# One exponential a tile in a decode kernel's attention, its weights spread to eight masked heads by a VectorE product

## The chip, the cores and the metric

The kernel runs on one core of a Trainium2 chip. The metric is the device time of one execution in microseconds. Engines are named as in the profile: PE is TensorE, DVE is VectorE, ACT is ScalarE, POOL is GpSimd, SP is SyncE, which here issues nearly all DMA transfers.

## What is computed

The kernel is one decode step for four sequences: a layernorm of x (4 x 640), attention over a cache, a small gated MLP beside it, and the sum of the three. All inputs and the output are bf16.

```python
xn = _layernorm(x)                                # x: 4 x 1 x 640
q = (xn @ wq).reshape(4, 1, 32, 128).transpose(0, 2, 1, 3)
scores = jnp.einsum('bhqd,bhkd->bhqk', q, k_cache) * 128 ** -0.5
p = softmax(scores)                               # over 4096 keys
o = jnp.einsum('bhqk,bhkd->bhqd', p, v_cache)     # caches: 4 x 32 x 4096 x 128
attn = o.transpose(0, 2, 1, 3).reshape(4, 1, 4096) @ wo
z = gelu(xn @ w_in); z1, z2 = z[..., :864], _layernorm(z[..., 864:])
mlp = (z1 * (w_sp * z2 + b_sp)) @ w_out
out = x + attn + mlp
```

Each of the 128 pairs of sequence and head has its own query, keys and values. The two caches are 134 MB each and are read once, so nearly all bytes (282 MB) are cache.

## The kernel before, in words

**Tiles.** A tile is eight heads of one sequence: 16 tiles (`NT`), in four head groups (`HG`) of four sequences (`Bsz`). A tile's K is 8 x 4096 rows of 128 numbers, laid out as 128 partitions ("lanes") with 256 rows each (`NC`), 8.39 MB; V is the same. A lane's 256 rows all belong to one head: 16 lanes (`LN`) for each of the eight heads (`HT`).

**Scores.** In tile i, K is worked on in four quarters (`NU`), each in four steps. `product(i, u)` (L402) multiplies a quarter in place on DVE by the lane's query, `fold(i, u)` (L411) adds its upper half of 64 columns to the lower, `sums(i, u)` (L420) adds the 64 columns up to 8 on PE by eight matmuls with an identity, and `row_sums(i, u)` (L431) adds the last 8 on DVE and writes 64 scores a lane into `s_sb`, a tile with **one** buffer. The query of the next tile is spread over the lanes by `stage_q` (L383, L388, L396).

**Softmax.** For tile i-1, during tile i: `lane_max` (L440) on DVE, `turn_max` (L445) on PE, `head_max` (L450) on DVE, `spread_max` (L461) on PE, and `bias` (L468) on DVE, which makes `nb`: for each lane eight numbers, the negative scaled maximum of head h, and -1e30 more (`off`) where the lane isn't of head h. `exps` (L480) then runs eight activations on ACT, one for each head, over all lanes: head h's weights are the exponentials on its own 16 lanes and zero on the other 112. They go to `pm[:, :, h]`, 128 lanes x 256 rows x 8 heads in bf16, so that one activation's outputs lie eight elements apart. Each also gives the row sum of its head (`accum_out`, into `acc`).

**Weighted values.** `weighted(i-1)` (L495) is 64 matmuls on PE: four rows by eight heads of `pm` are the weights, and four rows of V are the moving data; PE holds four groups of 32 columns. `take` (L505) copies the result on ACT, and `diag` (L515) picks with `pick` the pieces that belong together (a row's own position c among four and a head h: row c * 8 + h of the 32). `pm` has two buffers (pool `pmp`).

**After each group of four tiles.** `group_den` (L525, L529) adds the row sums over the lanes, `group_rows` (L533, L537) divides and spreads the rows over heads (`wide`), `group_turn` (L551, L559) transposes on PE. At the very end `group_proj` (L564) multiplies by `wo`, which was loaded last.

**What sets the order.** The order on PE, DVE, ACT and SP is the order of the calls in the loop (`manual_schedule`). K has two buffers, V one. In pass i of the loop SP issues V(i) (`load_v`, L128), which must wait until `weighted(i-1)` has read V(i-1), and after it K(i+2) (`load_k`, L122), which must wait until `sums(i, 3)` has read K(i). SP issues in order, and the transfers of its queue run in order. V of the last tile (`v_last`) goes into K's pool, and `wo` (L143) into V's.

Of the kernel before, what the change touches and what calls it, by code (L numbers as in the profile page):

```python
# [9 lines left out]
FP32 = mybir.dt.float32  # L10
BF16 = mybir.dt.bfloat16
ACT = mybir.ActivationFunctionType
ALU = mybir.AluOpType
AX = mybir.AxisListType

OFF = -1.0e30


@with_exitstack
def kernel(  # L20
# [14 lines left out]
    nc = tc.nc  # L35
    P = nc.NUM_PARTITIONS
    Bsz, Sq, D = A_x.shape
    _, H, S, Dh = A_k_cache.shape
# [4 lines left out]
    scale_qk = float(Dh) ** -0.5  # L43
# [3 lines left out]
    HT = 8  # L47
    HG = H // HT
    NT = HG * Bsz
    LN = P // HT  # L50
    NC = HT * S // P
# [17 lines left out]
    const = ctx.enter_context(tc.tile_pool(name="const", bufs=1))  # L69
    kp = ctx.enter_context(tc.tile_pool(name="kp", bufs=2))  # L70
    vp = ctx.enter_context(tc.tile_pool(name="vp", bufs=1))
    work = ctx.enter_context(tc.tile_pool(name="work", bufs=1))
    small = ctx.enter_context(tc.tile_pool(name="small", bufs=2))
    pmp = ctx.enter_context(tc.tile_pool(name="pmp", bufs=2))
    PSUM = bass.MemoryType.PSUM
    ps_s = ctx.enter_context(tc.tile_pool(name="ps_s", bufs=2, space=PSUM))
    ps_pv = ctx.enter_context(tc.tile_pool(name="ps_pv", bufs=2, space=PSUM))
# [7 lines left out]
    def v_slot(name):  # L85
# [21 lines left out]
        out=w_out_sb[:, 0:NFF, :], in_=B_w_out[0 : NFF * P].rearrange("(p k) n -> p k n", k=NFF)  # L107
# [42 lines left out]
    ident_f = const.tile([P, P], FP32)  # L150
# [5 lines left out]
    ones_col = const.tile([P, 1], FP32)  # L156
# [9 lines left out]
    for i in range(NSTAT):  # L166
# [9 lines left out]
        out=xn_bf,  # L176
        in0=x_bf,
        scalar1=mv[:, 0:1],
# [20 lines left out]
    for half in range(2):  # L199
# [6 lines left out]
        )  # L206


    off = const.tile([P, HT], FP32)
    nc.vector.tensor_reduce(  # L210
        out=off[:], in_=ident_f[:].rearrange("p (h l) -> p h l", h=HT), axis=AX.X, op=ALU.add
    )
    nc.vector.tensor_scalar(
        out=off[:], in0=off[:], scalar1=1.0, scalar2=-OFF, op0=ALU.subtract, op1=ALU.mult
    )
    nc.vector.tensor_reduce(
        out=pick[:, :, GW - HT : GW],
        in_=ident_f[:].rearrange("p (j c h) -> p c h j", c=CB, h=HT),
        axis=AX.X,
        op=ALU.add,  # L220
    )
    row_head = const.tile([ROWS, HT], FP32)
    nc.vector.tensor_reduce(
        out=row_head[:],
        in_=ident_f[:ROWS, :ROWS].rearrange("p (b h) -> p h b", h=HT),
        axis=AX.X,
        op=ALU.add,
    )
    row_batch_f = work.tile([ROWS, Bsz], FP32)
    nc.vector.tensor_reduce(  # L230
# [24 lines left out]

    GM = 2 * NFC * Bsz
    gm = {}
    gm_t = small.tile([P, 4 * GM + NFC * Bsz], FP32, tag="two_k", name="gm_t", bufs=1)
    for n, name in enumerate(("zz", "gw", "gt", "gz")):
        gm[name] = gm_t[:, n * GM : (n + 1) * GM].rearrange(  # L260
            "p (t k b) -> p t k b", t=2, b=Bsz
# [139 lines left out]
    def product(i, u):  # L401
        nc.vector.tensor_tensor(  # L402
            out=part(i, u),
            in0=part(i, u),
            in1=qbcs[i][:, None, :].to_broadcast([P, UC, Dh]),
            op=ALU.mult,
        )

    def fold(i, u):
        t = part(i, u)  # L410
        nc.vector.tensor_tensor(  # L411
            out=t[:, :, 0:HD2], in0=t[:, :, 0:HD2], in1=t[:, :, HD2:Dh], op=ALU.add
        )
# [50 lines left out]
        maxes[i] = nb_ps  # L464

    def bias(i):
        nb = small.tile([P, HT], FP32, name="nb")
        nc.vector.scalar_tensor_tensor(  # L468
            out=nb[:], in0=maxes[i][:], scalar=scale_qk, in1=off[:], op0=ALU.mult, op1=ALU.add
        )  # L470
        maxes[i] = nb

    def exps(i):
        hg, b = divmod(i, Bsz)
        if b == 0:
            accs[hg] = small.tile([P, Bsz, HT], FP32, name="acc")
        nb, s_sb, a = maxes.pop(i), scores.pop(i), accs[hg]
        pm = pms[i] = pmp.tile([P, NC, HT], BF16, tag="pm", name="pm")
        for h in range(HT):
            nc.scalar.activation(  # L480
                out=pm[:, :, h],
                in_=s_sb[:],
                func=ACT.Exp,
                bias=nb[:, h : h + 1],
                scale=scale_qk,
                accum_out=a[:, b, h : h + 1],
            )

    def weighted(i, c0=0, c1=NC):
        if c0 == 0:  # L490
            pvs[i] = ps_pv.tile([P, CB * Dh], FP32, tag="pv", name="pv")
        v_nat, pm = v_tiles[i], pms[i]
        for n in range(c0 // CB, c1 // CB):
            j = n % CG
            nc.tensor.matmul(  # L495
                out=pvs[i][j * GW : (j + 1) * GW, :],
                lhsT=pm[:, n * CB : (n + 1) * CB, :],
                rhs=v_nat[:, n * CB : (n + 1) * CB, :],
                start=(n < CG),
                stop=(n >= NB - CG),  # L500
            )

    def take(i):
        es[i] = small.tile([P, CB, Dh], FP32, tag="two_k", name="e", bufs=1)
        nc.scalar.copy(  # L505
            out=es[i][:], in_=pvs.pop(i)[:].rearrange("p (c d) -> p c d", d=Dh)
        )
# [13 lines left out]
            )  # L521

    def group_den(hg):
        den = ps_m.tile([ROWS, 1], FP32, tag="m", name="den")
        nc.tensor.matmul(  # L525
            out=den[:], lhsT=accs.pop(hg)[:], rhs=ones_col[:], start=True, stop=True
        )
        rdens[hg] = small.tile([ROWS, 1], FP32, name="rden")
        nc.vector.reciprocal(out=rdens[hg][:], in_=den[:])  # L529

    def group_rows(hg):
        o_n = small.tile([ROWS, Dh], BF16, name="o_n", bufs=1)
        nc.vector.tensor_scalar(  # L533
            out=o_n[:], in0=o_ps.pop(hg)[:], scalar1=rdens.pop(hg)[:], scalar2=None, op0=ALU.mult
        )
        wide = small.tile([ROWS, WJ, HT, LN], BF16, tag="two_k", name="wide", bufs=1)
        nc.vector.tensor_tensor(  # L537
            out=wide[:],
            in0=o_n[:].rearrange("r (m j) -> r j m", j=WJ)[:, :, None, :].to_broadcast(
                [ROWS, WJ, HT, LN]  # L540
            ),
            in1=row_head[:, None, :, None].to_broadcast([ROWS, WJ, HT, LN]),
            op=ALU.mult,
        )
        oTs[hg] = wide
# [26 lines left out]
    def at(i, fn, *args):  # L572
        if 0 <= i < NT:
            fn(i, *args)
# [6 lines left out]
    with tc.manual_schedule(engines={E.PE, E.DVE, E.Activation, E.SP}):  # L581
        stage_q(0)
        gmlp()
        load_v(0, v_slot("v_nat"))
        for i in range(NT):
            product(i, 0)
            fold(i, 0)
            at(i - 1, row_sums, NU - 1)
            at(i - 1, lane_max)
            group(i - 2, group_rows)  # L590
            sums(i, 0)
            at(i - 1, turn_max)
            group(i - 2, group_turn)
            product(i, 1)
            at(i - 1, head_max)
            at(i - 1, spread_max)
            fold(i, 1)
            at(i - 1, bias)
            at(i - 1, exps)
            at(i + 1, stage_q)  # L600
            sums(i, 1)
            row_sums(i, 0)
            product(i, 2)
            fold(i, 2)
            sums(i, 2)
            row_sums(i, 1)
            at(i - 1, weighted)
            if i == 0:
                pass
            elif i < NT - 1:  # L610
                load_v(i, v_slot("v_nat"))
            else:
                load_wo()
            at(i - 1, take)
            product(i, 3)
            fold(i, 3)
            sums(i, 3)
            row_sums(i, 2)
            if i + 2 < NT:
                load_k(i + 2)  # L620
            elif i + 2 == NT:
                load_v(NT - 1, k_slot("v_last"))
            at(i - 1, diag)
            group(i - 1, group_den)
        L = NT - 1
        row_sums(L, NU - 1)
        lane_max(L)
        group(L - 1, group_rows)
        turn_max(L)
        head_max(L)  # L630
        spread_max(L)
        bias(L)
        exps(L)
        for c0, c1 in zip(V_CUTS, V_CUTS[1:]):
            weighted(L, c0, c1)
        take(L)
        group_den(HG - 1)
        group_proj(0)
        diag(L)
        group_rows(HG - 1)  # L640
        group_proj(1)
        group_turn(HG - 1)
        group_proj(2)
        for j0, j1 in zip(WO_CUTS, WO_CUTS[1:]):
            group_proj(HG - 1, j0, j1)

        res = small.tile([P, NOH], BF16, tag="two_k", name="res", bufs=1)
        out_v = out.flatten_outer_dims()
        r0, r1 = slice(0, Bsz), slice(OG, OG + Bsz)
        nc.scalar.copy(out=res[r0], in_=out_ps[r0])  # L650
        nc.vector.tensor_copy(out=res[r1], in_=out_ps[r1])
        nc.scalar.dma_start(out=out_v[:, 0:NOH], in_=res[r0])
        nc.sync.dma_start(out=out_v[:, NOH:D], in_=res[r1])
# [30 lines left out]
```

## Time and profile before

| | us |
|---|---|
| three timed runs | 721.27, 718.67, 721.26; median 721.26 |
| the profiled execution, its own time | 722.45 |
| its span in the profile | 720.5 |
| busy: PE / PE weight loads / DVE / ACT / POOL | 310.7 / 129.2 / 491.3 / 172.7 / 1.0 |
| read from memory | 282.24 MB, 392 GB/s over the span |
| share of DMA queue 1 (that of SP) | 91.9% of 16 engines' span |

The span runs from the first to the last instruction of the program on the core; the execution's own time has some 2 us around it. Busy time counts an engine's instructions alone. A line of the groups reads: source line, engine, operation, output <- inputs with their shapes (partitions x elements) and how many; then busy us in all and mean ns of one; then the idle time ahead of them and what ended it. A line of the waits reads: who waited <- for whom: us in all, times, longest. A line of a time line reads: start us, us, engine, line, operation; in brackets the idle time ahead of it and what ended that. A line of windows has the stretch, its length, the busy time of each engine with its number of instructions, the granted PE clock, the DMA share and GB/s.

### The profile page before, as it was taken

What the parts mean: (1) busy time and instruction counts of PE and PEld (TensorE: products, weight loads), DVE (VectorE), ACT (ScalarE), POOL (GpSimd) and SP (SyncE); (2) the same over time, 40 slices, a digit from 0 to 9 for tenths busy, and PEclk for the clock granted to TensorE, in tenths of its full rate; (3) what the DMA queues carried; (4) which work ended last, traced back from release to release, by engine and by line L of the source; (5) the groups of instructions that cost most, each with busy time, mean ns of one, the idle gap of its engine ahead of it and who ended that gap; (6) DMA issues with size and microseconds to landing.
All of it is one profiled execution on the core that took longest, in us unless ns stands there. A gap on an engine that the chain in (4) does not pass through costs nothing.

```text
span 720.5 us, 4972 instructions
## 1 busy us (share of the span) xinstructions
PE 310.7 (43%) x2089; PEld 129.2 (18%) x2089; DVE 491.3 (68%) x291; ACT 172.7 (24%) x317; POOL 1.0 (0%) x8
## 2 busy tenths in 40 slices
PE   1513445252626327252634525272542617254256
PEld 1401112021202102020211202030120202022023
DVE  1259869474958849486876849497784849678441
ACT  0200130505041050503123050502205050320542
POOL 0000000000000000000000000000000000000000
PEclk9996558575866657585576758566575756767578
DMA  9999958999899997999899997999999897999981
GB/s 379 444 426 440 419 233 350 407 456 415 354 407 407 416 455 295 407 463 411 350 407 466 409 451 303 411 408 437 433 387 429 353 463 295 407 463 407 395 361 66
DMA packets 6498, 282.56 MB, mean 392 GB/s; under 512 B 736, under 2 KB 1100, under 8 KB 1484
## 3 DMA queue, kind: packets, MB, share of 16 engines
q1 hardware_dynamic: 6456, 282.24, 91.9%
q8 instruction: 16, 0.26, 0.1%
q14 instruction: 6, 0.05, 0.0%
q10 hardware_dynamic: 20, 0.01, 0.0%
HBM read 282.24 MB, written 0.01 MB: 392 GB/s over the span
## 4 chain that ended last, share of the span: by engine, by line
DVE 37%; DMA 34%; ACT 14%; PE 12%; issue 1%; SPq 0%; DVEq 0%
DMA k_nat<-in_A_k_cache_dram 34%; DVE k_nat L402 22%; ACT pm L480 14%; DVE k_nat L411 11%; PE s_ps L420 6%; PE pv L495 5%; DVE s_sb L431 3%; DVE wide L537 1%; DVE m L440 1%; PE out_ps L564 0%; PE o_ps L515 0%; DVE nm L450 0%; DVE o_n L533 0%; DVE nb L468 0%; SPq L109 0%
## 5 line engine op out<-in xcount | busy, mean ns | idle before, releaser
L402 DVE TENSOR_TENSOR k_nat<-k_nat,qbc 128x8192 bf16<-128x8192 bf16 x64 | 282.6, 4416 | 28.1 <-DMA k_nat<-in_A_k_cache_dram 28.1
L420 PE MATMUL s_ps<-k_nat,ident 128*128 128x512 bf16 x512 | 198.9, 559 | 181.3 <-DVE k_nat L411 181.3
L480 ACT ACTIVATE pm<-s_sb,nb 128x256 bf16<-128x256 f32 x128 | 149.8, 1582 | 223.3 <-DVE nb L468 223.3
L411 DVE TENSOR_TENSOR k_nat<-k_nat 128x4096 bf16<-128x4096 bf16 x64 | 146.4, 2287 | 1.7
L431 DVE TENSOR_REDUCE s_sb<-s_ps 128x64 f32<-128x512 f32 x64 | 43.9, 686 | 143.5 <-ACT pm L480 141.5
L420 PEld LDWEIGHTS <-ident 128*128 128x128 bf16 x512 | 65.2, 130 | 292.9 <-issue 264.0
L388 PE MATMUL qbc_ps<-ident,q_l 128*128 128x128 bf16 x16 | 4.5, 284 | 157.7 <-ACT q_l L383 157.7
L480 ACT ACTIVATION_READ_ACCUMULATOR pm<-s_sb,nb 128x1 f32 x128 | 63.0, 493 | 0.0
L505 ACT COPY e<-pv 128x512 f32<-128x512 f32 x16 | 9.4, 586 | 220.9 <-PE pv L495 215.3
L495 PE MATMUL pv<-v_nat,pm 128*32 128x512 bf16 x960 | 61.6, 414 | 0.0
L495 PEld LDWEIGHTS <-pm 128*32 128x32 bf16 x1024 | 27.2, 105 | 53.6 <-issue 23.9
L388 PEld LDWEIGHTS <-q_l 128*128 128x128 bf16 x16 | 1.7, 104 | 159.3 <-ACT q_l L383 159.1
L461 PE MATMUL nb_ps<-nm,ones_row 1*128 1x8 f32 x32 | 8.5, 336 | 35.9 <-DVE nm L450 35.9
L515 PE MATMUL o_ps<-e,pick 128*32 128x128 f32 x128 | 16.9, 275 | 0.0
L529 DVE RECIPROCAL rden<-den 32x1 f32<-32x1 f32 x4 | 0.6, 156 | 23.1 <-PE den L525 23.1
L461 PEld LDWEIGHTS nb_ps<-nm,ones_row 1*128 1x128 f32 x32 | 7.1, 275 | 44.2 <-DVE nm L450 29.8
L515 PEld LDWEIGHTS o_ps<-e,pick 128*32 128x32 f32 x128 | 12.8, 109 | 6.4 <-issue 6.4
L383 ACT COPY q_l<-qT 128x128 bf16<-128x128 bf16 x16 | 8.7, 543 | 17.4 <-DVE qT L251 17.4
L559 ACT CAST oT<-t_ps 128x32 bf16<-128x32 f32 x4 | 0.7, 186 | 45.2 <-PE t_ps L551 45.2
L396 ACT CAST qbc<-qbc_ps 128x128 bf16<-128x128 f32 x16 | 4.3, 266 | 29.1 <-PE qbc_ps L388 29.1
L251 DVE CAST qT<-q_ps 128x128 bf16<-128x128 f32 x1 | 0.3, 292 | 14.9 <-PE q_ps L243 14.9
L495 PE MATMUL pv<-v_last,pm 128*32 128x512 bf16 x64 | 5.5, 519 | 9.7 <-ACT pm L480 9.7
(81 smaller groups left out, 80.8 us busy)
## 6 DMA issues: line engine op xcount, KB each, us to landing
wq<-in_A_wq_dram SPq DMA_DIRECT2D x1, 5120.0 KB
v_last<-in_A_v_cache_dram SPq DMA_DIRECT2D x1, 4096.0 KB, 29.9
v_last<-in_A_v_cache_dram SPq DMA_DIRECT2D x2, 2048.0 KB, 34.5
wo<-in_A_wo_dram SPq DMA_DIRECT2D x3, 1280.0 KB
w_sb<-in_B_w_in_dram SPq DMA_DIRECT2D x1, 2160.0 KB, 20.1
w_sb<-in_B_w_out_dram SPq DMA_DIRECT2D x1, 960.0 KB, 22.6
wo<-in_A_wo_dram SPq DMA_DIRECT2D x1, 640.0 KB, 13.1
wo<-in_A_wo_dram SPq DMA_DIRECT2D x1, 320.0 KB, 11.9
```

The costliest lines, as they stand in the source:

```text
L383: nc.scalar.copy(out=q_l[:], in_=qT[:, HT * hg : HT * (hg + 1), b : b + 1].to_broadcast([P, HT, LN]),)
L402: nc.vector.tensor_tensor(out=part(i, u), in0=part(i, u), in1=qbcs[i][:, None, :].to_broadcast([P, UC, Dh]), op=ALU.mult,)
L411: nc.vector.tensor_tensor(out=t[:, :, 0:HD2], in0=t[:, :, 0:HD2], in1=t[:, :, HD2:Dh], op=ALU.add)
L420: nc.tensor.matmul(out=s[:], lhsT=ident[:], rhs=t[:, :, g * RW : (g + 1) * RW], start=(g == 0), stop=(g == n - 1),)
L431: nc.vector.tensor_reduce(out=scores[i][:, u * UC : (u + 1) * UC], in_=sums_ps.pop((i, u))[:], axis=AX.X, op=ALU.add,)
L440: nc.vector.tensor_reduce(out=m1[:], in_=scores[i][:], axis=AX.X, op=ALU.max)
L461: nc.tensor.matmul(out=nb_ps[:], lhsT=ones_row[:], rhs=maxes[i][:], start=True, stop=True)
L480: nc.scalar.activation(out=pm[:, :, h], in_=s_sb[:], func=ACT.Exp, bias=nb[:, h : h + 1], scale=scale_qk, accum_out=a[:, b, h : h + 1],)
L495: nc.tensor.matmul(out=pvs[i][j * GW : (j + 1) * GW, :], lhsT=pm[:, n * CB : (n + 1) * CB, :], rhs=v_nat[:, n * CB : (n + 1) * CB, :], sta ...
L505: nc.scalar.copy(out=es[i][:], in_=pvs.pop(i)[:].rearrange("p (c d) -> p c d", d=Dh))
L515: nc.tensor.matmul(out=o_ps[hg][:], lhsT=pick[:, c, GW - HT - HT * b : 2 * GW - HT - HT * b], rhs=e[:, c, :], start=(b == 0 and c == 0), s ...
L537: nc.vector.tensor_tensor(out=wide[:], in0=o_n[:].rearrange("r (m j) -> r j m", j=WJ)[:, :, None, :].to_broadcast([ROWS, WJ, HT, LN]), in1 ...
```

## The change

The lane-by-head mask moves from the exponential's bias to a product on DVE.

- The mask `own` (1 where the lane is of head h, else 0) takes the place of `off`. `own_c` is the same in bf16, each value four times.
- `bias` multiplies the eight maxima by `own` and adds them up (`accum_out`), which gives one number a lane: the maximum of its own head.
- `exps` is one activation over all lanes, into `p` (128 x 256 bf16, outputs in neighbouring elements), with one row sum a lane.
- `own_heads` is new: a DVE product of `p`, repeated for eight heads, and `own_c`, repeated for 64 blocks of four rows, into `pm`, now laid out as blocks x heads x four rows. In pass i it stands between `product(i, 2)` and `fold(i, 2)`, on DVE; at the end it follows the last exponential.
- `weighted` reads the four rows by eight heads of a block from neighbouring elements; `pick` follows the new order (row h * 4 + c of the 32).
- `group_den` spreads the lane's row sum over the heads with `own` before its matmul.
- `group_rows` writes `o_n` in the order in which `wide` reads it, and `row_head` is bf16 and spread over the 16 lanes once, at the start, so that `wide`'s product has bf16 operands in steps of one.
- The pool of `pm` goes from two buffers to one; the tiles of the tag `two_k` (`gm_t`, `e`, `wide`, `res`) go from one buffer to two.

The order of all other calls is as it was. On ACT 112 of 128 exponentials are gone; DVE has 21 instructions more; PE and SP have as many as before, in the same order.

```diff
-    pmp = ctx.enter_context(tc.tile_pool(name="pmp", bufs=2))
+    pmp = ctx.enter_context(tc.tile_pool(name="pmp", bufs=1))
...
-    nc.vector.tensor_scalar(
-        out=off[:], in0=off[:], scalar1=1.0, scalar2=-OFF, op0=ALU.subtract, op1=ALU.mult
-    )
+    own_c = const.tile([P, HT, CB], BF16)
+    nc.vector.tensor_copy(out=own_c[:], in_=own[:, :, None].to_broadcast([P, HT, CB]))
...
+    row_head = const.tile([ROWS, HT, LN], BF16)
+    nc.vector.tensor_copy(
+        out=row_head[:], in_=row_head_f[:, :, None].to_broadcast([ROWS, HT, LN])
     )
...
     def bias(i):
-        nb = small.tile([P, HT], FP32, name="nb")
+        nb = small.tile([P, 1], FP32, name="nb")
+        nb_h = small.tile([P, HT], FP32, name="nb_h")
         nc.vector.scalar_tensor_tensor(
-            out=nb[:], in0=maxes[i][:], scalar=scale_qk, in1=off[:], op0=ALU.mult, op1=ALU.add
+            out=nb_h[:],
+            in0=maxes[i][:],
+            scalar=scale_qk,
+            in1=own[:],
+            op0=ALU.mult,
+            op1=ALU.mult,
+            accum_out=nb[:],
         )
...
-        for h in range(HT):
-            nc.scalar.activation(
-                out=pm[:, :, h],
...
+        probs[i] = small.tile([P, NC], BF16, name="p")
+        nc.scalar.activation(
+            out=probs[i][:],
+            in_=scores.pop(i)[:],
+            func=ACT.Exp,
+            bias=maxes.pop(i)[:],
+            scale=scale_qk,
+            accum_out=accs[hg][:, b : b + 1],
+        )
+
+    def own_heads(i):
+        pm = pms[i] = pmp.tile([P, NB, HT, CB], BF16, tag="pm", name="pm")
+        nc.vector.tensor_tensor(
+            out=pm[:],
+            in0=probs.pop(i)[:]
+            .rearrange("p (n c) -> p n c", c=CB)[:, :, None, :]
+            .to_broadcast([P, NB, HT, CB]),
+            in1=own_c[:, None, :, :].to_broadcast([P, NB, HT, CB]),
+            op=ALU.mult,
+        )
...
-                lhsT=pm[:, n * CB : (n + 1) * CB, :],
+                lhsT=pm[:, n, :, :].rearrange("p h c -> p (h c)"),
...
     def group_den(hg):
+        acc = small.tile([P, Bsz, HT], FP32, name="acc_h", bufs=1)
+        nc.vector.tensor_tensor(
+            out=acc[:],
+            in0=accs.pop(hg)[:, :, None].to_broadcast([P, Bsz, HT]),
+            in1=own[:, None, :].to_broadcast([P, Bsz, HT]),
+            op=ALU.mult,
+        )
...
     def group_rows(hg):
         nc.vector.tensor_scalar(
-            out=o_n[:], in0=o_ps.pop(hg)[:], scalar1=rdens.pop(hg)[:], scalar2=None, op0=ALU.mult
-        )
-        wide = small.tile([ROWS, WJ, HT, LN], BF16, tag="two_k", name="wide", bufs=1)
+            out=o_n[:].rearrange("r (j m) -> r m j", j=WJ),
+            in0=o_ps.pop(hg)[:].rearrange("r (m j) -> r m j", j=WJ),
+            scalar1=rdens.pop(hg)[:], scalar2=None, op0=ALU.mult
+        )
+        wide = small.tile([ROWS, WJ, HT, LN], BF16, tag="two_k", name="wide")
...
-            in1=row_head[:, None, :, None].to_broadcast([ROWS, WJ, HT, LN]),
+            in1=row_head[:, None, :, :].to_broadcast([ROWS, WJ, HT, LN]),
...
             product(i, 2)
+            at(i - 1, own_heads)
             fold(i, 2)
...
         exps(L)
+        own_heads(L)
         for c0, c1 in zip(V_CUTS, V_CUTS[1:]):
             weighted(L, c0, c1)
```

More of the change, by code (lines that the diff above doesn't have):

```diff
@@ L14 @@
 AX = mybir.AxisListType
-OFF = -1.0e30
 @with_exitstack
@@ L206 @@
         )
-    off = const.tile([P, HT], FP32)
+    own = const.tile([P, HT], FP32)
     nc.vector.tensor_reduce(
-        out=off[:], in_=ident_f[:].rearrange("p (h l) -> p h l", h=HT), axis=AX.X, op=ALU.add
+        out=own[:], in_=ident_f[:].rearrange("p (h l) -> p h l", h=HT), axis=AX.X, op=ALU.add
     )
-    nc.vector.tensor_scalar(
-        out=off[:], in0=off[:], scalar1=1.0, scalar2=-OFF, op0=ALU.subtract, op1=ALU.mult
-    )
+    own_c = const.tile([P, HT, CB], BF16)
+    nc.vector.tensor_copy(out=own_c[:], in_=own[:, :, None].to_broadcast([P, HT, CB]))
     nc.vector.tensor_reduce(
         out=pick[:, :, GW - HT : GW],
-        in_=ident_f[:].rearrange("p (j c h) -> p c h j", c=CB, h=HT),
+        in_=ident_f[:].rearrange("p (j h c) -> p c h j", c=CB, h=HT),
         axis=AX.X,
@@ L221 @@
     )
-    row_head = const.tile([ROWS, HT], FP32)
+    row_head_f = work.tile([ROWS, HT], FP32)
     nc.vector.tensor_reduce(
-        out=row_head[:],
+        out=row_head_f[:],
         in_=ident_f[:ROWS, :ROWS].rearrange("p (b h) -> p h b", h=HT),
@@ L257 @@
     gm = {}
-    gm_t = small.tile([P, 4 * GM + NFC * Bsz], FP32, tag="two_k", name="gm_t", bufs=1)
+    gm_t = small.tile([P, 4 * GM + NFC * Bsz], FP32, tag="two_k", name="gm_t")
     for n, name in enumerate(("zz", "gw", "gt", "gz")):
@@ L466, in bias @@
     def bias(i):
-        nb = small.tile([P, HT], FP32, name="nb")
+        nb = small.tile([P, 1], FP32, name="nb")
+        nb_h = small.tile([P, HT], FP32, name="nb_h")
         nc.vector.scalar_tensor_tensor(
-            out=nb[:], in0=maxes[i][:], scalar=scale_qk, in1=off[:], op0=ALU.mult, op1=ALU.add
+            out=nb_h[:],
[5 more added lines that the diff above has]
+            accum_out=nb[:],
         )
         maxes[i] = nb
+    probs = {}
     def exps(i):
@@ L475, in exps @@
         if b == 0:
-            accs[hg] = small.tile([P, Bsz, HT], FP32, name="acc")
-        nb, s_sb, a = maxes.pop(i), scores.pop(i), accs[hg]
-        pm = pms[i] = pmp.tile([P, NC, HT], BF16, tag="pm", name="pm")
-        for h in range(HT):
-            nc.scalar.activation(
-                out=pm[:, :, h],
[L482 to L486, printed above, removed]
-            )
+            accs[hg] = small.tile([P, Bsz], FP32, name="acc")
+        probs[i] = small.tile([P, NC], BF16, name="p")
[17 more added lines that the diff above has]
+        )
     def weighted(i, c0=0, c1=NC):
@@ L503, in take @@
     def take(i):
-        es[i] = small.tile([P, CB, Dh], FP32, tag="two_k", name="e", bufs=1)
+        es[i] = small.tile([P, CB, Dh], FP32, tag="two_k", name="e")
         nc.scalar.copy(
@@ L523, in group_den @@
     def group_den(hg):
+        acc = small.tile([P, Bsz, HT], FP32, name="acc_h", bufs=1)
[5 more added lines that the diff above has]
+        )
         den = ps_m.tile([ROWS, 1], FP32, tag="m", name="den")
         nc.tensor.matmul(
-            out=den[:], lhsT=accs.pop(hg)[:], rhs=ones_col[:], start=True, stop=True
+            out=den[:], lhsT=acc[:], rhs=ones_col[:], start=True, stop=True
         )
@@ L533, in group_rows @@
         nc.vector.tensor_scalar(
-            out=o_n[:], in0=o_ps.pop(hg)[:], scalar1=rdens.pop(hg)[:], scalar2=None, op0=ALU.mult
+            out=o_n[:].rearrange("r (j m) -> r m j", j=WJ),
+            in0=o_ps.pop(hg)[:].rearrange("r (m j) -> r m j", j=WJ),
+            scalar1=rdens.pop(hg)[:], scalar2=None, op0=ALU.mult
         )
-        wide = small.tile([ROWS, WJ, HT, LN], BF16, tag="two_k", name="wide", bufs=1)
+        wide = small.tile([ROWS, WJ, HT, LN], BF16, tag="two_k", name="wide")
         nc.vector.tensor_tensor(
             out=wide[:],
-            in0=o_n[:].rearrange("r (m j) -> r j m", j=WJ)[:, :, None, :].to_broadcast(
+            in0=o_n[:].rearrange("r (j m) -> r j m", j=WJ)[:, :, None, :].to_broadcast(
                 [ROWS, WJ, HT, LN]
             ),
-            in1=row_head[:, None, :, None].to_broadcast([ROWS, WJ, HT, LN]),
+            in1=row_head[:, None, :, :].to_broadcast([ROWS, WJ, HT, LN]),
             op=ALU.mult,
@@ L645 @@
             group_proj(HG - 1, j0, j1)
-        res = small.tile([P, NOH], BF16, tag="two_k", name="res", bufs=1)
+        res = small.tile([P, NOH], BF16, tag="two_k", name="res")
         out_v = out.flatten_outer_dims()
```

## The prediction

> **What bounds the kernel now.** I read the groups, the waits, one tile's time line, then the DMA queue. The groups give the prices on VectorE (DVE):
>
> ```profile
> L402 DVE TENSOR_TENSOR k_nat<-k_nat,qbc 128x8192 bf16<-128x8192 bf16 x64 | 282.6, 4416 | 28.1 <-DMA k_nat<-in_A_k_cache_dram 28.1
> L480 ACT ACTIVATE pm<-s_sb,nb 128x256 bf16<-128x256 f32 x128 | 149.8, 1582 | 223.3 <-DVE nb L468 223.3
> L411 DVE TENSOR_TENSOR k_nat<-k_nat 128x4096 bf16<-128x4096 bf16 x64 | 146.4, 2287 | 1.7
> L431 DVE TENSOR_REDUCE s_sb<-s_ps 128x64 f32<-128x512 f32 x64 | 43.9, 686 | 143.5 <-ACT pm L480 141.5 <-PE s_ps L420 1.9
> ```
>
> DVE works 30.5 us a tile (four times 4.42 + 2.29 + 0.69, and small ones), and its one large wait stands ahead of `row_sums(i, 0)`: 141.5 us for the exponentials of L480. The scores tile `s_sb` has one buffer, so the first sums of tile i can't be written until all eight exponentials of tile i-1 have read it. The time line of VectorE in tile 7 shows that wait:
>
> ```profile
> 335.25 0.15 DVE L468 SCALAR_TENSOR_TENSOR nb<-nb_ps,off 128x8 f32<-128x8 f32 x1
> 344.82 0.69 DVE L431 TENSOR_REDUCE s_sb<-s_ps 128x64 f32<-128x512 f32 x1 [9.43 <-ACT pm L480]
> 345.43 4.42 DVE L402 TENSOR_TENSOR k_nat<-k_nat,qbc 128x8192 bf16<-128x8192 bf16 x1
> ```
>
> So a tile takes DVE about 30.5 + 9.43 = 40 us. Beside it runs the DMA queue, whose own waits and issues (time line of SP) are these:
>
> ```profile
> SPq L128 <- PE pv L495: 272.8, 14, 28.7
> ```
> ```profile
> 609.80 0.33 SPq L128 DMA_DIRECT2D v_nat<-in_A_v_cache_dram  x1
> 611.61 0.33 SPq L122 DMA_DIRECT2D k_nat<-in_A_k_cache_dram  x1
> 649.85 0.33 SPq L128 DMA_DIRECT2D v_nat<-in_A_v_cache_dram  x1
> ```
>
> V has one buffer: V(i) is issued when `weighted(i-1)` has left PE, and K(i+2) stands behind it on SP. V(1) is issued at 111.44 and V(14) at 649.85, so a tile now takes 538.4 / 13 = 41.4 us. How fast the DMA could go, windows of 12 us tell (the last two columns are DMA share and GB/s):
>
> ```profile
> 322.00:334.00 12.00, 4.38 (x11) 1.61 (x10) 11.93 (x7) 0.00 (x0) 0.00 (x0) 0.55 1.01 437
> 334.00:346.00 12.00, 1.05 (x4) 0.50 (x5) 2.57 (x4) 9.73 (x18) 0.00 (x0) 0.50 1.01 437
> ```
>
> 437 GB/s with VectorE busy for 11.93 us and with it idle for most: VectorE's work doesn't slow the transfers. One K or V is 8.39 MB, 19.2 us at that rate. The landing records agree: K(7) at 320.70, V(6) at 340.06, K(8) at 359.44, so 38.7 us a pair. The 41.4 of today are 38.7 plus holes: V(7) is issued at 360.18, after K(8) has landed, and from such a late issue a V takes about 21.8 us to land, 2.4 more. Where V is issued ahead of K's landing by 4.1 or 4.9 us (V(6), V(2)) it lands 19.4 and 19.2 after K; with a lead of 2.6 (V(8)) 20.8; with 1.4 (V(10)) 21.9. **So DMA is nearly the bound already, and VectorE with its stall makes the holes.**
>
> **The change, part by part.** Times in the profiled execution: span 720.5, its own time 722.45, which is 1.2 above the median 721.26.
>
> 1. Eight exponentials become one. The stall was 9.43. One ACTIVATE of this shape takes 1.43 alone (at 335.43, the first of its eight). Below: the copies on ACT take 0.27 to 0.59, with the 0.49 of the accumulator's read 0.76. Above: 1.43 + 0.49 = 1.92. I take 1.45. The Trainium skill (ScalarE: Activation LUTs, What ACT_TABLE_LOAD costs) gives 280 ns + 0.833 ns an element, so an estimate of 0.49; no run so far shows the exponential with neighbouring outputs, and by it the forecast would be 1 to 2 us lower.
>
> 2. `own_heads` adds a VectorE product of 128x2048 a tile. From L402 and L411, both bf16 in steps of one: (4416 - 2287) / 4096 = 0.52 ns an element and 158 ns fixed, so 0.158 + 2048 x 0.52 = 1.22 us. Its runs are only four elements long, and no row has that. The other end is `wide` (L537), 1951 ns for 1024 elements with a strided input and an f32 one: 3.9 us. Below 1.1 there is no reason to go. I take 1.22, since all three operands are bf16 in steps of one as in L402. The Trainium skill (Vector Engine (DVE) Microarchitecture Reference, 5.1 Performance modes) asks, for two results a cycle, for 2-byte types, innermost steps of one and more than one element in the innermost row: four would do. Its table for 2048 elements has 1224 ns; by the rival row the sum would be some 7 us longer, below.
>
> 3. `bias` gets an accumulator: L468 is 0.148 now; the only accumulator read in the trace (ACT) is 0.49. I take 0.1 more, between 0 and 0.5.
>
> So the gain in the path of VectorE is 9.43 - 1.45 - 1.22 - 0.1 = **6.7 us a tile** (3.5 to 7.6).
>
> 4. One weight buffer: `own_heads(i-1)` must wait for `weighted(i-2)`, which left PE before V(i-1) was issued, one tile earlier. That is over 20 us ahead, so 0; behind a wait there, `fold(i, 2)` and all that follows on VectorE would stand. The weights on PE read neighbouring elements now; PE's loads are 0.1 us each as before, so 0.
>
> 5. The setup's two casts run ahead of the cast of L251, where VectorE waits 14.9 us for PE: 0. `acc_h` in `group_den` is some 0.2 us, four times, three under the slack below. `wide` becomes bf16 in steps of one: 0.158 + 1024 x 0.52 = 0.69 in place of 1.95, 1.3 less at the end. The second buffers of `two_k` take away waits of which the trace shows none.
>
> **The sum.** V(i) is issued 38.6 to 39.4 us after the tile's first product (tile 3: 154.83 to 193.41; tile 7: 320.79 to 360.18), 40.6 in tile 9 with group work. Less 6.7 this is 32 to 34, and K(i+1) lands 38.7 after K(i): a lead of 5 to 7 us, more than the 4.1 that sufficed. VectorE's 32 us a tile are below 38.7 as well. So the gain of 6.7 isn't had in full: **DMA becomes the bound, and a tile goes from 41.4 to about 38.8.**
>
> - V(1): nothing hides the gain in tile 1. Issue 111.44 - 6.7 = 104.7, landing 21.8 later, 126.5.
> - From there to K(15): K(3), V(2), K(4) ... V(13), K(15), 25 transfers of 19.4 = 485, so 611.5 (651.81 today). At 19.25: 607.8; at 19.6: 616.5.
> - From K(15) to the end, 68.7 today: V(14) and `v_last` 38.8; `wo` behind them, in 13.8 at most (today from 693.6, 2.3 after its issue, to 707.46), 12.0 at 437 GB/s; then two matmuls, the copy of 0.5 and the store's 2.2: 53.5 to 55.4. The compute chain gives 68.7 - 6.7 - 6.7 - 1.3 = 54.0 (the stall of the last loop pass, the last tile's exponentials, `wide`). I take 55.
>
> Span 611.5 + 55 = 666.5; own time 1.95 more, 668.4; median 1.2 less: **667 us**.
>
> The Trainium skill (HBM Reference, Specifications) speaks against a gain: it gives a core about 358 GB/s of its memory's share, and about 425 when it streams alone. By the first a pair would take an estimate of 47 us, and DMA would allow nothing below today's time. The trace, with 437 in 12 us and 392 over the span, is on the side of the second.
>
> **Rivals.**
>
> - *The product runs at the rate of `wide`* (3.9 us). For it: the short runs. V(1) comes 2.7 later, the leads shrink to 2.3 to 4.3 and open holes of a few tenths to 1.3 in some tiles (some 2 us in all), and the end is 2.7 later: about 675. Chance 0.10.
> - *The transfers don't run back to back.* V from a late start and its K need 39 to 41 us after the latency in today's trace; if pairs average 39.8, 12.5 x 1 = 12 more: 679. Against it are the pairs of 38.6 (K(3) to K(4)) and 38.7. Chance 0.11.
> - *VectorE takes the stall back, and more* (the other side). If the product with four-element runs costs over 1.22 + 6.7 = 8 us, 3.9 ns an element and twice the slowest row, VectorE is the bound as before, and each us above it costs one a tile: at 10 us 16 x 2, so about 750. Or the wait ahead of L431 isn't for the exponentials' read, and stays: 721 + 16 x 1.3 = 742. Against: the wait ends with L480 in 15 of 15. Chance of both 0.04.
> - In between, with 7 to 8 us, no change: 0.01.
> - *Shorter still*: an exponential of 0.76 and 19.2 a transfer: 657 to 659. Chance 0.04.
>
> The forecast (659 to 674) has 0.70. The range 658 to 682 takes in the first two rivals and the bounds of the product; it leaves out the shortest case and those with no gain. A measurement of this kernel can tell 0.5%, 3.6 us, from no change: faster 0.95, same 0.01, slower 0.04.
>
> **What would show it.** In the profile after: L431's wait on ACT falls from 9.4 to some 1.5 a tile; the new product stands at about 1.2 us; VectorE's wait for K grows from 28.1 to 80 or more; each V is issued 5 to 7 us before the K ahead of it lands; the GB/s row loses its holes (mean 392 to about 423); the last chain is mostly DMA. Wrong I would be if the product is over 4 us, or if the pair of transfers takes 40 us though V is issued early.

## The result and the profile after

| | before | after |
|---|---|---|
| median | 720.2 us (718.7 to 721.3, four runs) | 669.8 us (668.9 to 670.2, four runs) |
| ratio | | 0.930, 95% interval 0.928 to 0.932 |
| profiled execution, its span / own time | 720.5 / 722.45 | 667.8 / 669.53 |
| mean GB/s over the span | 392 | 423 |

The kernel became 7% faster; 667 was forecast. The page of the kernel after shows first where a DMA queue without holes can be seen: the share of its 16 engines and the GB/s in 40 slices.

```profile
DVE  1239999939689596968969596996949699695971
ACT  0200000000000000000000000000000000000000
...
DMA  9999997999999999999999999999999999999996
GB/s 372 448 437 440 417 412 315 440 437 440 433 436 416 416 441 436 436 433 440 437 432 436 437 420 433 432 424 433 440 437 432 436 440 425 432 436 425 418 417 263
...
q1 hardware_dynamic: 6456, 282.24, 98.2%
```

One slice still dips, the seventh (315), where V(1) comes late. Here three slices stand below 400, the first and the last among them; before, it was thirteen:

```profile
GB/s 379 444 426 440 419 233 350 407 456 415 354 407 407 416 455 295 407 463 411 350 407 466 409 451 303 411 408 437 433 387 429 353 463 295 407 463 407 395 361 66
```

The groups of the kernel after (L403, L412, L432 and L488 are the old L402, L411, L431 and L480; L499 is the new product):

```profile
L403 DVE TENSOR_TENSOR k_nat<-k_nat,qbc 128x8192 bf16<-128x8192 bf16 x64 | 282.7, 4417 | 100.3 <-DMA k_nat<-in_A_k_cache_dram 100.3
...
L432 DVE TENSOR_REDUCE s_sb<-s_ps 128x64 f32<-128x512 f32 x64 | 43.8, 685 | 11.4 <-ACT p L488 10.0
...
L488 ACT ACTIVATE p<-s_sb,nb 128x256 bf16<-128x256 f32 x16 | 8.1, 507 | 279.1 <-DVE nb_h L470 279.1
...
L499 DVE TENSOR_TENSOR pm<-p,own_c 128x2048 bf16<-128x2048 bf16 x16 | 19.5, 1219 | 0.7 <-ACT p L488 0.7
```

VectorE's large wait has changed its name. It no longer stands ahead of the row sums for ACT (141.5 us then, 10.0 now), but ahead of the first product for K: 28.1 then, 100.3 now. The row sums wait 0.67 a tile, as the time line of pass 7 shows:

```profile
316.11 0.15 DVE L470 SCALAR_TENSOR_TENSOR nb_h<-nb_ps,own 128x8 f32<-128x8 f32 x1
316.20 0.07 DVE L470 DVE_READ_ACCUMULATOR nb_h<-nb_ps,own 128x1 f32 x1
316.30 0.51 ACT L488 ACTIVATE p<-s_sb,nb 128x256 bf16<-128x256 f32 x1 [20.93 <-DVE nb_h L470]
316.72 0.19 ACT L488 ACTIVATION_READ_ACCUMULATOR p<-s_sb,nb 128x1 f32 x1
...
316.94 0.69 DVE L432 TENSOR_REDUCE s_sb<-s_ps 128x64 f32<-128x512 f32 x1 [0.67 <-ACT p L488]
```

And the DMA queue's own waits (SP) in the kernel after:

```profile
SPq L126 <- DMA v_nat<-in_A_v_cache_dram: 322.1, 14, 28.9
SPq L126 <- PE pv L514: 178.2, 14, 21.2
```

V's issue waited 272.8 us for the weights' matmuls before, 178.2 now; the rest of its wait is for the V ahead of it to land, which costs nothing. V(1) is still issued 1.9 us after K(2) has landed (104.0 and 102.2). From V(2) on, V(i) is issued 5.5 to 11.7 us before the K ahead of it lands, and DMA runs with hardly a break: of the 25 transfers from the landing of V(1) to that of K(15), 23 take 19.34 to 19.37 us by the trace's landing records (a transfer has landed with the last of its 16). K(3), right behind the late V(1), takes 20.8, and K(12) 20.9, for which no cause is known (e10 has 20.8 there too).

The chain of work that ended last, by engine, first before and then after:

```profile
DVE 37%; DMA 34%; ACT 14%; PE 12%; issue 1%; SPq 0%; DVEq 0%
```
```profile
DMA 54%; DVE 33%; PE 11%; ACT 1%; issue 1%; SPq 1%; DVEq 0%
```

It is mostly DMA now, as forecast. Most of VectorE's third of it is steps that lead to an issue of K, and that transfer then stands in a queue that still has 20 us of work or more; e8 below tests whether an earlier issue would bring anything.

### The profile page after: what moved, and what is told of

Same layout as the page of the kernel before. It is cut to its first block, busy times and chain, and to the rows that moved or that the text cites. A ratio compares the mean times of both kernels' runs of the same rounds, so it can differ in the third digit from the quotient of the medians.

```text
span 667.8 us, 4772 instructions
## 1 busy us (share of the span) xinstructions
PE 312.8 (47%) x2089; PEld 128.7 (19%) x2089; DVE 505.9 (76%) x328; ACT 33.6 (5%) x93; POOL 1.0 (0%) x8
## 4 chain that ended last, share of the span: by engine, by line
DMA 54%; DVE 33%; PE 11%; ACT 1%; issue 1%; SPq 1%; DVEq 0%
DMA k_nat<-in_A_k_cache_dram 51%; DVE k_nat L403 19%; DVE k_nat L412 9%; PE s_ps L421 6%; PE pv L514 4%; DMA wo<-in_A_wo_dram 2%; DVE s_sb L432 2%; DVE pm L499 1%; ACT p L488 1%; PE out_ps L592 1%; DVE m L441 1%; DVE wide L565 0%; DVE o_n L559 0%; DVE nm L451 0%; SPq L141 0%
## 5 line engine op out<-in xcount | busy, mean ns | idle before, releaser
L403 DVE TENSOR_TENSOR k_nat<-k_nat,qbc 128x8192 bf16<-128x8192 bf16 x64 | 282.7, 4417 | 100.3 <-DMA k_nat<-in_A_k_cache_dram 100.3
L421 PE MATMUL s_ps<-k_nat,ident 128*128 128x512 bf16 x512 | 201.6, 565 | 257.4 <-DVE k_nat L412 257.4
L412 DVE TENSOR_TENSOR k_nat<-k_nat 128x4096 bf16<-128x4096 bf16 x64 | 146.2, 2285 | 1.2
L432 DVE TENSOR_REDUCE s_sb<-s_ps 128x64 f32<-128x512 f32 x64 | 43.8, 685 | 11.4 <-ACT p L488 10.0
L488 ACT ACTIVATE p<-s_sb,nb 128x256 bf16<-128x256 f32 x16 | 8.1, 507 | 279.1 <-DVE nb_h L470 279.1
L499 DVE TENSOR_TENSOR pm<-p,own_c 128x2048 bf16<-128x2048 bf16 x16 | 19.5, 1219 | 0.7 <-ACT p L488 0.7
L252 DVE CAST qT<-q_ps 128x128 bf16<-128x128 f32 x1 | 0.3, 292 | 14.8 <-PE q_ps L244 14.8
L555 DVE RECIPROCAL rden<-den 32x1 f32<-32x1 f32 x4 | 0.6, 156 | 12.5 <-PE den L551 12.5
L244 PE MATMUL q_ps<-xnT,wq 128*128 128x4 bf16 x160 | 4.4, 166 | 11.1 <-DMA wq<-in_A_wq_dram 11.1
L592 PE MATMUL out_ps<-wo,oT 128*4 128x320 bf16 x64 | 6.4, 363 | 1.7 <-DMA wo<-in_A_wo_dram 1.7
L441 DVE TENSOR_REDUCE m<-s_sb 128x1 f32<-128x256 f32 x16 | 6.7, 420 | 0.6
L244 PEld LDWEIGHTS <-wq 128*128 128x128 bf16 x160 | 4.3, 104 | 11.5 <-DMA wq<-in_A_wq_dram 11.5
```

The costliest lines, as they stand in the source:

```text
L403: nc.vector.tensor_tensor(out=part(i, u), in0=part(i, u), in1=qbcs[i][:, None, :].to_broadcast([P, UC, Dh]), op=ALU.mult,)
L412: nc.vector.tensor_tensor(out=t[:, :, 0:HD2], in0=t[:, :, 0:HD2], in1=t[:, :, HD2:Dh], op=ALU.add)
L421: nc.tensor.matmul(out=s[:], lhsT=ident[:], rhs=t[:, :, g * RW : (g + 1) * RW], start=(g == 0), stop=(g == n - 1),)
L432: nc.vector.tensor_reduce(out=scores[i][:, u * UC : (u + 1) * UC], in_=sums_ps.pop((i, u))[:], axis=AX.X, op=ALU.add,)
L441: nc.vector.tensor_reduce(out=m1[:], in_=scores[i][:], axis=AX.X, op=ALU.max)
L488: nc.scalar.activation(out=probs[i][:], in_=scores.pop(i)[:], func=ACT.Exp, bias=maxes.pop(i)[:], scale=scale_qk, accum_out=accs[hg][:, b ...
```

## The experiments

The theory: VectorE lost 9.4 us a tile, because the one scores buffer tied it to eight slow exponentials; that made V's issue late and holes in the DMA queue. The change takes the stall away, DMA becomes the bound at 38.8 us a tile, and what the change adds on VectorE is hidden in every pass but the first and the last. The rivals: another part of the change brought the gain (neighbouring weights, `wide`, ACT's light load); or VectorE is the bound still. Each ratio below is to the kernel before, run again beside the experiment (medians 721.2 to 723.2).

### Take away the wait, keep the eight exponentials (e1, e10)

```diff
-    pmp = ctx.enter_context(tc.tile_pool(name="pmp", bufs=2))
+    pmp = ctx.enter_context(tc.tile_pool(name="pmp", bufs=1))
...
-            scores[i] = small.tile([P, NC], FP32, name="s_sb", bufs=1)
+            scores[i] = small.tile([P, NC], FP32, name="s_sb", bufs=2)
```

> The kernel before with its eight exponentials, but two buffers for the scores tile s_sb, and one for the weights pm to make room. Theory (the stall of VectorE behind the exponentials was the loss, and DMA is the next bound): the wait of row_sums(i, 0) for ACT goes from 141.5 us to about 0; V(1) is issued about 9.4 us sooner, near 102; pairs of transfers take 38.8; the last tile's eight exponentials and the slow wide stay in the end, so about 59 us from the landing of K(15) to the end in place of 55 in the changed kernel. About 671 us (668 to 675). Rival (the gain came from ACT's lighter load, the neighbouring weights on PE or the faster wide): 715 to 721, as before. A second rival (one weight buffer costs a wait of the exponentials for weighted): some us a tile, 690 or more.

Measured: 680.8 us, ratio 0.944 (0.940 to 0.948). Most of the gain, but 6 us short of the range. Its groups say that VectorE still waits at the same line, only for another engine:

```profile
L431 DVE TENSOR_REDUCE s_sb<-s_ps 128x64 f32<-128x512 f32 x64 | 43.6, 682 | 86.5 <-PE s_ps L420 86.5
```

The time line of e1 tells why. ACT runs its queue in order, and the copy of the next tile's query (L383) stands behind the eight exponentials; on PE the matmul on it (L388) stands ahead of the eight of `sums(i, 1)`:

```profile
329.98 0.49 ACT L480 ACTIVATION_READ_ACCUMULATOR pm<-s_sb,nb 128x1 f32 x1
330.00 0.58 ACT L383 COPY q_l<-qT 128x128 bf16<-128x128 bf16 x1
...
330.63 0.29 PE L388 MATMUL qbc_ps<-ident,q_l 128*128 128x128 bf16 x1 [11.50 <-ACT q_l L383]
...
333.96 0.69 DVE L431 TENSOR_REDUCE s_sb<-s_ps 128x64 f32<-128x512 f32 x1 [5.74 <-PE s_ps L420]
```

So the stall had two ways to VectorE, and the second became visible with the first gone. The follow-up issues the query first:

```diff
             at(i - 1, spread_max)
             fold(i, 1)
+            at(i + 1, stage_q)
             at(i - 1, bias)
             at(i - 1, exps)
-            at(i + 1, stage_q)
```

> As e1 (two scores buffers, one weight buffer, eight exponentials), with the next tile's query (stage_q) issued on ACT and PE ahead of bias and the exponentials. In e1 VectorE's wait had moved: ACT's copy of the query stood behind the eight exponentials, PE's matmul on it stood ahead of sums(i, 1), and row_sums(i, 0) waited 86.5 us for PE; V(1) was issued at 106.3. Theory (that queue is what was left): the 86.5 goes, V(1) is issued near 102, passes are bound by DMA, and from K(15) to the end it is 59 as in e1: 670 to 673 us. Rival (eight exponentials slow something else, such as the weights' matmuls or the transfers): 677 or more, near e1's 680.8.

Measured: 672.0 us, ratio 0.930 (0.927 to 0.933), inside the range. V(1) is issued at 101.46. The groups of e10:

```profile
L402 DVE TENSOR_TENSOR k_nat<-k_nat,qbc 128x8192 bf16<-128x8192 bf16 x64 | 282.5, 4414 | 118.8 <-DMA k_nat<-in_A_k_cache_dram 118.8
...
L480 ACT ACTIVATE pm<-s_sb,nb 128x256 bf16<-128x256 f32 x128 | 150.9, 1595 | 43.1 <-DVE nb L468 43.1
...
L431 DVE TENSOR_REDUCE s_sb<-s_ps 128x64 f32<-128x512 f32 x64 | 43.5, 680 | 1.7 <-PE s_ps L420 1.7
```

All 128 exponentials are there at their old price, 150.9 us on ACT, with the weights still eight elements apart, without the mask product and without `wide`'s new form, and the gain is the same within the intervals. What was won was VectorE's wait, not ACT's work. Only behind the last tile does the cheap exponential count for itself: from the landing of K(15) to the end e10 takes 58.9 us and the changed kernel 55.0. In e10 V(1) is issued 2.6 us sooner, which makes up for most of that. The one weight buffer of e1 and e10 makes no wait either: ACT's only wait ahead of L480 is for `nb`.

### Keep the wait, make the exponentials cheaper (e2)

```diff
-        pm = pms[i] = pmp.tile([P, NC, HT], BF16, tag="pm", name="pm")
+        pm = pms[i] = pmp.tile([P, NB, HT, CB], BF16, tag="pm", name="pm")
...
-                out=pm[:, :, h],
-                in_=s_sb[:],
+                out=pm[:, :, h, :],
+                in_=s_sb[:].rearrange("p (n c) -> p n c", c=CB),
```

`weighted` and `pick` follow the new layout as in the changed kernel.

> The kernel before with its eight exponentials a tile on one scores buffer, but the weights laid out as blocks x heads x four rows, so that an exponential writes runs of four neighbouring elements. Theory (an exponential of 1.13 us a step was slow because its outputs lie eight elements apart; the changed kernel's one takes 0.51): eight take 4 to 5 us, the stall falls from 9.4 to 4.3, V's issue has a lead of some 4 us, and the time comes near the changed kernel: 673 to 680. Rival (each activation has a fixed price of 1.1 us, whatever its output steps): stall 9.4, 715 to 721. If runs of four are no better than single elements, the same.

Measured: 681.2 us, ratio 0.944 (0.941 to 0.947), one us above the range. The groups of e2:

```profile
L480 ACT ACTIVATE pm<-s_sb,nb 128x256 bf16<-128x256 f32 x128 | 63.1, 494 | 262.7 <-DVE nb L468 262.7
L431 DVE TENSOR_REDUCE s_sb<-s_ps 128x64 f32<-128x512 f32 x64 | 43.9, 686 | 63.0 <-ACT pm L480 61.6
```

The same 128 exponentials, with outputs in runs of four in place of single elements eight apart, take 494 ns in place of 1582, one starts every 0.49 us in place of 1.13, and the stall is 61.6 / 15 = 4.1 us a tile in place of 9.4. The price of an exponential here was the step of its output; a fixed price of 1.1 us an activation is refuted. With the stall at 4.1 four of the V's from V(2) on are issued less than 4.5 us ahead (V(5) 2.5 us before K(6) lands, V(7) 4.4, V(9) 1.8, V(13) 3.8), where none is in the changed kernel, and from V(1) to K(15) a transfer takes 19.8 us in place of 19.5.

### How much VectorE's cover holds (e3, e4)

```diff
+        p = probs.pop(i)
+        for _ in range(4):
             nc.vector.tensor_tensor(
                 out=pm[:],
...
```

e4 has 8 for 4.

> The changed kernel with the product of own_heads issued four times, 3.7 us more a tile on VectorE. Theory (DMA is the bound, VectorE has a lead of 4 to 9 us): nearly all passes hide most of it; V(1) comes 3.7 later, the leads fall to 0.5 to 5.8 and holes of up to 2 us open in some tiles, so 675 to 684. Rival (VectorE bounds the passes still): 16 x 3.7 = 59 more, 729.

> The changed kernel with the product of own_heads issued eight times, 8.5 us more a tile, 9.8 in all. Theory (the product breaks even with the old stall at about 8 us): V is issued later than in the kernel before, and VectorE is the bound with some 40.5 us a tile: 725 to 735, slower than before. Rival (DMA's slack is larger than the traces say): 700 or less.

Measured: e3 685.5 us, ratio 0.948 (0.945 to 0.952); e4 728.9 us, ratio 1.010 (1.006 to 1.014). e3 lies 1.5 above its range: of 16 x 3.7 = 59 us more work 16 show. Its span is 16.8 longer than the changed kernel's: V(1) lands 3.1 later, the transfers up to K(15) take 8.8 more, and the rest behind K(15) 4.9 more. e4 lies in its range, and is 1% slower than the kernel before. So the point from which the product takes back all the gain lies between 4.9 and 9.8 us a tile, the product's times in e3 and e4. A straight line between the two runs puts it near 9, an estimate, where 8 was expected. VectorE's wait for K and the product in e4:

```profile
L403 DVE TENSOR_TENSOR k_nat<-k_nat,qbc 128x8192 bf16<-128x8192 bf16 x64 | 282.6, 4416 | 19.1 <-DMA k_nat<-in_A_k_cache_dram 18.5
L501 DVE TENSOR_TENSOR pm<-p,own_c 128x2048 bf16<-128x2048 bf16 x128 | 156.7, 1224 | 4.6 <-ACT p L488 0.7
```

The wait for K, 100.3 in the changed kernel, is the cover; at 18.5 it is spent.

### The steps of one, and wide (e7, e9)

e7 has the heads innermost in the weights (`own_c`, `pick` and `weighted` follow), so that the product reads each exponential eight times in a step of zero:

```diff
-            in0=probs.pop(i)[:]
-            .rearrange("p (n c) -> p n c", c=CB)[:, :, None, :]
-            .to_broadcast([P, NB, HT, CB]),
+            in0=probs.pop(i)[:]
+            .rearrange("p (n c) -> p n c", c=CB)[:, :, :, None]
+            .to_broadcast([P, NB, CB, HT]),
```

> The changed kernel with the weights laid out as blocks x four rows x heads, so that in the product the heads are innermost and the exponential's operand is read eight times in a step of zero. Theory (what made the product cheap is that all three operands step by one): the product takes 2.3 us (one element a cycle) to 3.9 us (as wide before) in place of 1.22; passes hide it; V(1) and the last tile come 1.1 to 2.7 later: 671 to 675 us. Rival (steps don't matter for a product of this size): 1.22 us and 669 to 670.

Measured: 671.1 us, ratio 0.928 (0.925 to 0.930). The product of e7:

```profile
L499 DVE TENSOR_TENSOR pm<-p,own_c 128x2048 bf16<-128x2048 bf16 x16 | 36.6, 2285 | 0.7 <-ACT p L488 0.7
```

2285 ns against 1219: the steps of one nearly halve the product, 17 us over the kernel, and the time moves by about 1 us, within the spread of the runs: the passes hide it. The Trainium skill (Vector Engine (DVE) Microarchitecture Reference, 5.1 Performance modes) says that a two-source product which reads one element again and again goes at one element a cycle, and one with rows in steps of one at two; the trace agrees with both, 2285 and 1219 ns for 2048.

e9 undoes `wide`, with `row_head` and the order in `o_n`, and the second buffers of `two_k`:

```diff
-        wide = small.tile([ROWS, WJ, HT, LN], BF16, tag="two_k", name="wide")
+        wide = small.tile([ROWS, WJ, HT, LN], BF16, tag="two_k", name="wide", bufs=1)
...
-            in1=row_head[:, None, :, :].to_broadcast([ROWS, WJ, HT, LN]),
+            in1=row_head[:, None, :, None].to_broadcast([ROWS, WJ, HT, LN]),
```

> The changed kernel with wide, row_head and the order in o_n as in the kernel before, and one buffer for the tag two_k (the weights keep their one buffer). Theory (wide's 1.3 us lie beside the landing of wo at the end and beside the DMA slack in the passes): 670 to 671.3. Rival (these parts are a good share of the gain): 675 or more.

Measured: 668.7 us, ratio 0.927 (0.924 to 0.930), no difference from the changed kernel. These parts bring nothing.

### Take bytes away (e5, e6)

```diff
-    V_CUTS = (0, NC // 2, 3 * NC // 4, NC)
+    NV = NC // 2
+    V_CUTS = (0, NV // 2, 3 * NV // 4, NV)
...
-        cuts = V_CUTS if i == NT - 1 else (0, NC)
+        cuts = V_CUTS if i == NT - 1 else (0, NV)
...
-    def weighted(i, c0=0, c1=NC):
+    def weighted(i, c0=0, c1=NV):
```

The same edit in both kernels; the end of each sum on PE (`stop`) moves with it.

> The kernel before, loading and weighting only the first half of V's rows in each tile: the second half of the attention's sum is left out. DMA has 29 us of work a tile in place of 38.7. Theory (before the change VectorE with its stall was the pace, 39.3 us a pass, and DMA only made it a little longer): 15 passes of 39.3 and the ends, about 696, only 3% less. Rival (DMA was the bound before the change): with a quarter of the bytes gone about 600 or less.

> The changed kernel, loading and weighting only the first half of V's rows in each tile: the second half of the attention's sum is left out. Theory (DMA is the bound now, with VectorE at 31.9 us a pass behind it): VectorE becomes the bound: 72.6 + 15 x 31.9 + 3 for the groups, and 17.6 at the end: about 572, 15% less than the changed kernel. Rival (VectorE is still the pace after the change): 660 or more.

Measured: e5 703.7 us, ratio 0.974 (0.969 to 0.979); e6 576.3 us, ratio 0.798 (0.794 to 0.802). e5 is 8 us above its forecast and e6 4, but the two theories are told from their rivals by far more. With a quarter of the bytes gone the kernel before gains 18 us (722.1 to 703.7 on the same chip), since VectorE with its stall needs nearly as long as ever; the changed kernel gains 93. In e5 the stall is untouched:

```profile
L432 DVE TENSOR_REDUCE s_sb<-s_ps 128x64 f32<-128x512 f32 x64 | 43.8, 685 | 142.9 <-ACT pm L481 141.5 <-PE s_ps L421 1.4
```

and VectorE waits for K only once, for the first tile. Its first products stand 39.2 us apart, and 41.5 to 41.7 in two passes of each four, with the work at the end of a group; the forecast of 39.3 for every pass left these out. The stretch from 200 to 500 us in e5 and then in e6 (length, busy PE, weight loads, DVE, ACT, POOL, then PE clock, DMA share, GB/s):

```profile
200.00:500.00 300.00, 120.54 (x562) 46.60 (x561) 218.55 (x117) 82.35 (x153) 0.00 (x0) 0.64 0.74 315
```
```profile
200.00:500.00 300.00, 152.32 (x722) 59.17 (x720) 286.75 (x166) 15.32 (x48) 0.00 (x0) 0.70 0.90 384
```

In e6 VectorE is busy for 287 of 300 us: it is the next bound, at about 32 us a tile (31.4 from one first product to the next, and 32.8 to 34.0 with the work at the end of a group). In e5 it is busy for 219; seven or eight stalls of 9.4 behind the exponentials are some 70 more, so busy time and stall fill the stretch, while DMA is down to 0.74.

### A version that beats both (e8)

If DMA is the bound, only its holes are left to win, and the one that stands is V(1)'s: K(2) lands at 102.2, V(1) is issued at 104.0. e8 spreads and uses the weights earlier in each pass:

```diff
             row_sums(i, 0)
+            at(i - 1, own_heads)
+            at(i - 1, weighted)
             product(i, 2)
-            at(i - 1, own_heads)
             fold(i, 2)
             sums(i, 2)
             row_sums(i, 1)
-            at(i - 1, weighted)
```

> The changed kernel with own_heads ahead of product(i, 2) and weighted(i-1) ahead of sums(i, 2) on PE, so that V(i) is issued some 8 us sooner in each pass. Theory (DMA bounds all passes but the first, where V(1) is issued at 104.0 while K(2) has landed at 101.8): only the hole ahead of V(1) goes; V(1) lands at 121.2 in place of 125.9; all after it moves by that: 664 to 666 us, faster by 4 to 5. Rival (VectorE or PE still sets the pace of the passes): faster by much more than 5, or, if weighted holds up sums(i, 2), slower than 670.

Measured: 663.6 us, ratio 0.920 (0.917 to 0.922), clear of the changed kernel's 0.928 to 0.932; 0.4 us below the range. The stretch from 97 to 113 us, first in the kernel after, then in e8 (last column GB/s):

```profile
97.00:113.00 16.00, 12.00 (x94) 4.83 (x93) 15.90 (x8) 0.59 (x1) 0.00 (x0) 0.82 0.68 280
```
```profile
97.00:113.00 16.00, 7.93 (x28) 3.16 (x27) 15.90 (x9) 0.03 (x1) 0.00 (x0) 0.82 1.03 443
```

V(1) is issued at 96.4 and lands at 121.8, 4.2 us sooner than the 126.0 of the kernel after (the 121.2 and 125.9 of the expectation were worked out from the issue). K(3) lands at 141.1 in place of 146.7, 5.6 sooner: behind a V that was issued in time it takes 19.4 and not 20.8, and this 1.4 is what the expectation missed. From there the difference stays: K(15) lands 5.7 sooner, the last piece of `wo` 5.6 (658.5 and 664.1), and the span is 6.0 shorter. Every later V is issued some 8 us sooner too, and `wo` at 631.6 in place of 643.8, and neither brings anything more: `wo` ends 12.5 us after the last V in both. This is what a bound by DMA looks like.

## Why the prediction was right

- *The stall goes, and VectorE waits for K instead.* Right: 141.5 to 10.0 us, and 28.1 to 100.3 ("80 or more"). e1, e2 and e10 show that the wait is the cause, each by another way to shorten it.
- *The exponential at 1.45 us.* Too high: one takes 0.51, and VectorE waits 0.67. This is the term that was mis-sized most. The row it was taken from, 1.43, has outputs eight elements apart; e2 shows that this step was the price. The Trainium skill (ScalarE: Activation LUTs, What ACT_TABLE_LOAD costs) had it: its 0.49 stands beside 0.494 in e2 and 0.507 after; the 1.58 of the kernel before, with outputs eight elements apart, does not follow it. The error made VectorE's gain 7.5 us a tile in place of 6.7 (9.43 - 0.67 - 1.22 - 0.07). It was worth 0.7 us in V(1)'s issue, 104.0 for 104.7. Elsewhere the leads hid it: they were put at 5 to 7 us and are 5.5 to 11.7.
- *The product at 1.22.* Right: 1.219. Runs of four are as good here as the long rows of L403. The rival at 3.9 had the wrong row. Its price was put at 8 us for 2.7 more a tile, of which 2 in holes; e3, with 3.7 more, cost 16, of which 8.8 up to K(15), so the cover is somewhat thinner than was thought.
- *The accumulator of bias at 0.1.* Right in size: its read takes 0.07.
- *DMA at 19.4 a transfer.* Nearly right: from V(1), landing at 126.0 (126.5), to K(15), at 612.7 (611.5), it is 486.7 for 25, so 19.5. These 1.7 us more, less the 0.5 of V(1), are the 1.2 by which the span came out longer than forecast (667.8 for 666.5). All of it lies in K(3) and K(12), which took 1.4 and 1.5 longer than the 19.35 of the other 23. The rival with 39.8 a pair fell.
- *The lead that suffices.* The prediction reads a lead of 2.6 us and 20.8 for V(8). By the landing records that is V(11), with 20.6; V(8) leads by 4.0 us and lands 19.4 after K(9). The rule drawn from it, that some 4 us suffice, stands (last section).
- *From K(15) to the end 55.* Right: 667.8 - 612.7 = 55.1. With `wide` at its old price it is no longer (e9).
- *The point from which it would be slower, some 8 us.* Roughly right: it lies between 4.9 and 9.8, near 9 by the estimate above. With the measured exponential the same sum gives 8.7 (9.43 - 0.67 - 0.07). Its price was too high: at 10 us 750 was forecast, and e4 took 728.9 at 9.8.
- *One weight buffer, the setup, two_k at nothing.* Right: the product (L499) has only 0.7 us of idle time ahead of it in all, the wait of the cast at L252 for PE is 14.8 (14.9 before), and e9 shows nothing for `two_k`.
- *What wasn't seen:* that the stall had a second way to VectorE, by ACT's copy of the query and PE's queue (e1). The change removes both, since its exponential takes 0.5 us, so that the forecast didn't suffer. Had the buffer alone been the change, the forecast of e1 would have missed by 10 us, as the expectation of e1 did.
- The median is 2.8 us above the forecast: 1.2 by the span; 669.53 - 667.8 = 1.7 around it in place of 1.95; and the 1.2 by which the profiled execution of before stood over its median, which was subtracted here, didn't come again (669.53 against 669.78). That correction lies within the spread of the runs.

## What to carry to other kernels

Before an engine's work is made cheaper, ask who waits for it: here 112 of 128 exponentials went, and the same gain is had with all of them by a second buffer of 1 KB a lane (the weights gave up one of theirs for it) and one call in another place. Follow such a stall through every in-order queue behind it; a second buffer frees one way, and the next one shows. When a bound is near (DMA at 92% of its time), price the gain by that bound's own pace, and then look only for its remaining holes, as e8 did.

## What the runs showed of the hardware that was not expected

- ACT takes more than twice as long when its bf16 outputs lie eight elements apart: 256 exponentials a lane start every 1.13 us, against 0.49 in runs of four. What follows on ACT is slower as well: the accumulator's read takes 0.49 in place of 0.19, and the copy of the query behind the last exponential 577 ns in place of 281.
- A transfer must be issued some us ahead of the landing before it to follow without a gap. The landing records of all runs with the whole of V (all but e5 and e6) give the limit. Every whole V issued 4.45 us or more ahead of a K's landing landed 19.2 to 19.7 us after it, but for one at 20.2 (e7). Those issued less than 4 us ahead took 19.5 to 22.6. Between 4.0 and 4.45 both occur: 19.4 at 4.0 (V(8) before), 20.7 at 4.4 (V(7) in e2). Where V is issued after the landing, it takes 21.7 to 22.0 from its issue, but for one at 23.3 (e4).
- A late V can cost twice: K(3) behind a V(1) that was issued less than 1 us ahead of K(2)'s landing or after it took 19.7 to 21.4 us in all nine of these runs, and 19.4 in e8, where V(1) was 6 us ahead. Behind other late V's K takes 19.4 in some cases and up to 20.9 in others; why isn't known.
